# One input block loaded on a hardware queue, and index tables built on Pool, in a fused linear-attention and gated-FFN kernel

## The chip, the cores and the metric

The kernel runs on one core of a Trainium2 chip. The metric is the device time of one execution in microseconds (us), taken as the median of several executions. The span in a profile, from the first to the last instruction, is about 1.8 us shorter than that time.

Names in profile lines: PE is the matmul engine (TensorE) and PEld its weight loads, DVE is VectorE, ACT is ScalarE, POOL is GpSimd, SP is SyncE. An engine's name with a "q" behind it (SPq, ACTq, POOLq) is its sequencer, for instance where it issues a DMA. L115 is line 115 of that kernel; lines shift by a few from one kernel to the next.

## The reference

The reference does linear attention with a decay per head, followed by a gated feed-forward layer. B is 4, H is 8, S is 768 and D is 64; inputs and output are fp32.

```
for each block of the sequence:
    intra = (q_b @ k_b^T * Dmask) @ v_b          # Dmask[i,j] = lam^(i-j) for i >= j, else 0
    inter = (q_b * lam^(pos+1)) @ kv_state
    out_b = intra + inter
    kv_state = lam^block * kv_state + (k_b * lam^(block-1-pos))^T @ v_b

x    = out, transposed to (B*S, H*D) = (3072, 512)
gate = sigmoid(x @ w_gate)                       # 512 -> 1536
val  = x @ w_val
y    = (gate * val) @ w_out                      # 1536 -> 512
```

The kernel works in bf16 with fp32 sums, and in six steps of 128 positions ("step 0" is the block 0 of the change).

## The kernel before

The start is what the change touches. Pool issues nearly all loads, and its DMA casts fp32 to bf16 on the way. The q of batches 0 and 1 goes another way: it comes as fp32 over the hardware queues of ScalarE and Sync, and an engine casts it afterwards. VectorE builds the index tables (`ip1`, 1 to 128 along the row, and `p1`, 1 to 128 down the partitions) by doubling, a transpose and four offset adds.

```python
    lam1 = const.tile([1, H], FP32, tag="lam1")
    nc.sync.dma_start(out=lam1, in_=lam.partition_broadcast(1))
    # ... cut: weights' tiles, load() and load_w(), which issue casting DMAs on Pool ...
    q01 = [const.tile([128, H, D], FP32, tag=f"q{b}f", name=f"q{b}f") for b in range(2)]
    nc.scalar.dma_start(out=q01[0], in_=q[0, :, 0:C, :].rearrange("h s d -> s h d"))
    nc.sync.dma_start(out=q01[1], in_=q[1, :, 0:C, :].rearrange("h s d -> s h d"))
    # ... cut: tiles ...
    nc.vector.memset(ip1[:, 0:1], 1.0)
    w = 1
    while w < C:
        nc.vector.tensor_scalar_add(ip1[:, w:2 * w], ip1[:, 0:w], float(w))
        w *= 2
    loc = const.tile([128, 32], FP32, tag="loc")
    nc.vector.transpose(loc, ip1[:, 0:32])
    p1 = const.tile([128, 1], FP32, tag="p1")
    for lo in range(0, 128, 32):
        nc.vector.tensor_scalar_add(p1[lo:lo + 32], loc[lo:lo + 32, 0:1], float(lo))
    # ... cut: jn, ident, tri from ip1 and p1 ...
    load(0, "k", 0, 2)
    load(0, "k", 2, 4)
    load(0, "q", 2, 3)
    load(0, "q", 3, 4)
    load(0, "v", 0, 1)
    # ... cut: more v, gate and value weights, in the order of need ...
```

TensorE begins with filler matmuls (`idle(n)`), which keep it busy while it waits for data, and then does step 0: it transposes q and k (`piece_tq0`, `piece_tk0`), multiplies them (`piece_s`), VectorE masks the product (`piece_m`), and so on until the first gate matmul. The output stores all go out on Sync. The stores of step 0 are cut in two parts for some tiles, and the last tile of all is stored in two unequal parts, so that the very last store carries only 64 KB:

```python
    def piece_po(n, tt):
        # ... cut: 12 matmuls into po ...
        nc.scalar.copy(ob, po)
        parts = 2 if n == 0 and tt < 2 else 1
        rows = 128 // parts
        for i in range(parts):
            lo = tt * S + n * C + i * rows
            nc.sync.dma_start(out=out[lo:lo + rows, :], in_=ob[i * rows:(i + 1) * rows, :])

    def piece_last(n, tt):
        # ... cut: for columns 0 to 384 and 384 to 512: matmuls; ScalarE copies the first part, VectorE the second ...
            nc.sync.dma_start(out=out[tt * S + n * C:tt * S + (n + 1) * C, lo:hi], in_=ob[:, lo:hi])
```

Of the kernel before, what the change touches and what calls it, by code (L numbers as in the profile page):

```python
# [7 lines left out]
FP32 = mybir.dt.float32  # L8
BF16 = mybir.dt.bfloat16
# [6 lines left out]
def kernel(  # L16
# [11 lines left out]
    nc = tc.nc  # L28

    B, H, S, D = q.shape  # L30
    C = 128
# [9 lines left out]
    const = ctx.enter_context(tc.tile_pool(name="const", bufs=1))  # L41
    qkv = ctx.enter_context(tc.tile_pool(name="qkv", bufs=4))
# [26 lines left out]
    Q, K, V = {}, {}, {}  # L69

    def load(n, what, b0, b1):
        sl = slice(n * C, (n + 1) * C)
        for c in what:
            lst, src = {"q": (Q, q), "k": (K, k), "v": (V, v)}[c]
            if n > 1 and c != "v":
                lst[n] = qkv.tile([128, 2, B, HP, D], BF16, tag=c + "b", name=c + "b")
                for e in range(2):
                    nc.gpsimd.dma_start(  # L78
                        out=lst[n][:, e].rearrange("p b y d -> p (b y) d"),
                        in_=src[:, e::2, sl, :].rearrange("b y s d -> s (b y) d"))  # L80
                continue
            if n == 1 and c != "v":
                if n not in lst:
                    lst[n] = qkv.tile([128, 2, B * H * D // 2], BF16, tag=c + "b", name=c + "b")
                if b0 == 0:
                    nc.gpsimd.dma_start(
                        out=lst[n][:, 0].rearrange("p (x d) -> p x d", d=D),
                        in_=src[b0:b1, :, sl, :].rearrange("b h s d -> s (b h) d"))
                else:
                    for e in range(2):  # L90
                        nc.gpsimd.dma_start(
                            out=lst[n][:, 1].rearrange("p (e x d) -> p e x d", e=2, d=D)[:, e],
                            in_=src[b0:b1, e::2, sl, :].rearrange("b y s d -> s (b y) d"))
                continue
            if n not in lst:
                lst[n] = qkv.tile([128, B, H, D], BF16, tag=c + "b", name=c + "b")
            nc.gpsimd.dma_start(  # L97
                out=lst[n][:, b0:b1],
                in_=src[b0:b1, :, sl, :].rearrange("b h s d -> s (b h) d"))
# [13 lines left out]
    q01 = [const.tile([128, H, D], FP32, tag=f"q{b}f", name=f"q{b}f") for b in range(2)]  # L113
    nc.scalar.dma_start(out=q01[0], in_=q[0, :, 0:C, :].rearrange("h s d -> s h d"))
    nc.sync.dma_start(out=q01[1], in_=q[1, :, 0:C, :].rearrange("h s d -> s h d"))  # L115
    Q[0] = qkv.tile([128, B, H, D], BF16, tag="qb", name="qb")
    nc.scalar.preload_act_table_set("natural_log_exp_and_others")
    ident = const.tile([128, 128], BF16, tag="ident")
# [2 lines left out]
    ip1 = const.tile([128, C], FP32, tag="ip1")  # L121
# [2 lines left out]
    nc.vector.memset(zero, 0.0)  # L124
    nc.vector.memset(ones, 1.0)
    Sb = stp.tile([128, B, HP, D], BF16, tag="Sb", name="Sb")
    nc.vector.memset(ip1[:, 0:1], 1.0)
    w = 1
    while w < C:
        nc.vector.tensor_scalar_add(ip1[:, w:2 * w], ip1[:, 0:w], float(w))  # L130
        w *= 2
    loc = const.tile([128, 32], FP32, tag="loc")
    nc.vector.transpose(loc, ip1[:, 0:32])
    p1 = const.tile([128, 1], FP32, tag="p1")
    for lo in range(0, 128, 32):
        nc.vector.tensor_scalar_add(p1[lo:lo + 32], loc[lo:lo + 32, 0:1], float(lo))
    for i, base in enumerate((0.0, float(C))):
        nc.vector.tensor_scalar(out=jn[:, i:i + 1], in0=p1, scalar1=-1.0, scalar2=base,
                                op0=ALU.mult, op1=ALU.add)
    nc.vector.tensor_scalar(out=ident, in0=ip1, scalar1=p1, scalar2=None, op0=ALU.is_equal)  # L140
    nc.vector.tensor_scalar(out=tri, in0=ip1, scalar1=p1, scalar2=None, op0=ALU.is_ge)

    load(0, "k", 0, 2)
    load(0, "k", 2, 4)
    load(0, "q", 2, 3)
    load(0, "q", 3, 4)
# [12 lines left out]
    def idle(n):  # L159
        for i in range(n):  # L160
            nc.tensor.matmul(wm, lhsT=zero[:, :C], rhs=zero, start=True, stop=True,
                             skip_group_check=True)

    idle(4)
    lamp = ps_at.tile([128, H], FP32, name="lamp", tag="ps")
    nc.tensor.matmul(lamp, lhsT=ones, rhs=lam1, start=True, stop=True)
    lnl = const.tile([128, H], FP32, tag="lnl")
# [9 lines left out]
    pk = const.tile([128, H], FP32, tag="pk")  # L177
    nc.scalar.activation(pk, lnl, AF.Exp, scale=jn[:, 0:1])
    nc.scalar.copy(Q[0][:, 1], q01[1])
    kds = const.tile([128, H], FP32, tag="kds")  # L180
    nc.scalar.activation(kds, lnl, AF.Exp, scale=jn[:, 1:2])
    dec = const.tile([128, HP], FP32, tag="dec")
# [21 lines left out]
    def make_mask(u):  # L204
        nc.vector.tensor_tensor(
            out=mask[:, u::2, :], in0=tri.unsqueeze(1).to_broadcast([128, HP, C]),
            in1=pk[:, u::2].unsqueeze(2).to_broadcast([128, HP, C]), op=ALU.mult)
# [42 lines left out]
    def transpose_pair(out, x, b, g):  # L250
        nc.tensor.transpose(out, x[:, b, 2 * g:2 * g + 2, :].rearrange("p h d -> p (h d)"), ident)
# [7 lines left out]
    def piece_tq0(bs, then=None):  # L259
        tq = ps_at.tile([128, 2, 2, 2 * C], BF16, name="tq", tag="ps")  # L260
        for b in bs:
            if (0, b // 2) not in QS:
                QS[0, b // 2] = trsb.tile([128, 2, 2, 2, C], BF16, tag="QS", name="QS")
            for g in range(HP):
                transpose_pair(tq[:, b % 2, g // 2, g % 2 * C:g % 2 * C + C], Q[0], b, g)
        if then:
            then()
        for b in bs:
            nc.vector.tensor_tensor(out=QS[0, b // 2][:, :, b % 2].rearrange("p e x c -> p e (x c)"),
                                    in0=tq[:, b % 2], in1=lamq0_e, op=ALU.mult)  # L270

    def piece_tk0(bp):
        tk = ps_at.tile([128, 2, 2, 2 * C], BF16, name="tk", tag="ps")
        for i in range(2):
            for g in range(HP):
                transpose_pair(tk[:, i, g // 2, g % 2 * C:g % 2 * C + C], K[0], 2 * bp + i, g)
        KS[0, bp] = trsb.tile([128, 2, 2, 2, C], BF16, tag="KS", name="KS")
        for i in range(2):
            cp = nc.vector.tensor_copy if bp == 0 and i == 0 else nc.scalar.copy
            cp(KS[0, bp][:, :, i].rearrange("p e x c -> p e (x c)"), tk[:, i])  # L280
# [20 lines left out]
    def piece_s(n, bs, pool=ps_at, tag="ps"):  # L301

        for b in bs:
            bp, i = b // 2, b % 2
            sp = [pool.tile([128, HP, C], FP32, name=f"sp{u}", tag=tag) for u in range(2)]
            for hp in range(HP):
                for u in range(2):
                    us = slice(u * 64, (u + 1) * 64)
                    nc.tensor.matmul(sp[u][:, hp, :], lhsT=KS[n, bp][us, hp // 2, i, hp % 2, :],  # L309
                                     rhs=QS[n, bp][us, hp // 2, i, hp % 2, :],  # L310
                                     start=(hp == 0), stop=(hp == HP - 1), skip_group_check=True)
            SP[n, b] = sp
# [176 lines left out]
    def piece_po(n, tt):  # L489
        po = ps_ff.tile([128, DM], FP32, name="po", tag="ff")  # L490
        for ft in range(NFT):
            nc.tensor.matmul(po, lhsT=HT[n, ft][:, tt * 128:(tt + 1) * 128],  # L492
                             rhs=WO[:, ft, :], start=(ft == 0), stop=(ft == NFT - 1))
        ob = osb.tile([128, DM], FP32, tag="ob", name="ob")
        nc.scalar.copy(ob, po)  # L495
        parts = 2 if n == 0 and tt < 2 else 1
        rows = 128 // parts
        for i in range(parts):
            lo = tt * S + n * C + i * rows
            nc.sync.dma_start(out=out[lo:lo + rows, :], in_=ob[i * rows:(i + 1) * rows, :])  # L500
# [2 lines left out]
    load_gv(1, GW)  # L503
    load_gv(2, GW)

    idle(6)
    nc.vector.tensor_copy(Q[0][:, 0], q01[0])
    piece_tq0([0])
    make_mask(0)
    idle(1)  # L510
    piece_tq0([1])
    piece_tk0(0)
    make_mask(1)
    idle(1)
    piece_s(0, [0])
    piece_m(0, 0)
    piece_s(0, [1])
# [111 lines left out]
    load(3, "qkv", 0, B)  # L629
    gvh(1, 1, *range(NFT))  # L630
    piece_po(0, 0)
    piece_po(0, 1)
    piece_po(0, 2)
    t(2, 0)
    t(2, 1)
# [72 lines left out]
```

## Time and profile before

| | before |
|---|---|
| median of 3 runs | 227.5 us (227.39 to 227.57) |
| span of the profiled run | 225.7 us |
| TensorE busy | 218.7 us, 97% |
| k transposes of step 0 start | 7.48 us |
| first masked eviction (VectorE) starts | 9.08 us |
| first gate matmul starts | 15.04 us |
| end of the last PSUM copy to end of span | 2.66 us |

The list of waits of TensorE in the kernel before has four entries that are no small change. The columns are the instruction that waited, what released it, us in total, times, longest.

```profile
PE wm L161 <- DVE zero L124: 1.2, 1, 1.2
PE tk L251 <- DMA kb<-in_k_dram: 0.7, 1, 0.7
PE tq L251 <- DMA qb<-in_q_dram: 0.5, 1, 0.5
PE sp L309 <- DMA KR<-kb: 0.4, 1, 0.4
```

The timeline of the kernel before shows where these lie. The columns are start, duration, engine, line, operation, output and inputs, count, and in brackets the idle time before it and what ended it.

```profile
1.26 2.43 POOL L97 DMA_DIRECT2D kb<-in_k_dram  x2 [0.81 <-POOLq L692]
1.32 2.61 DVE L130 TENSOR_SCALAR ip<-ip 128x1 f32<-128x1 f32 x7
...
7.48 0.62 PE L251 MATMUL tk<-ident,kb 128*128 128x128 bf16 x8 [0.70 <-DMA kb<-in_k_dram]
...
9.08 2.48 DVE L211 TENSOR_TENSOR MT<-sp,mask 128x512 bf16<-128x512 f32 x4
...
15.04 0.81 PE L443 MATMUL gp<-XT,WG 128*128 128x384 bf16 x4
...
74.41 0.62 PE L309 MATMUL sp<-QS,KR 64*128 64x128 bf16 x16 [0.42 <-DMA KR<-kb]
```

VectorE spends 2.61 us on the seven doubling adds. TensorE waits 0.70 us for the k that Pool loads. After 17 us it waits once, for the transposed k of step 2 at 74.41 us.

The DMA view of the kernel before, for 4 to 5 us and for 7 to 8 us, shows a dip and the full rate. A packet of these loads reads 256 bytes; it writes 128 as bf16 on Pool's queue (q0) and 256 as fp32 on Sync's (q1).

```profile
DMA packets 547, 0.08 MB, mean 85 GB/s; under 512 B 547, under 2 KB 547, under 8 KB 547
...
q0 software_dynamic: 414, 0.05, 82.6%
q1 hardware_dynamic: 133, 0.03, 20.8%
```

```profile
DMA packets 1233, 0.16 MB, mean 157 GB/s; under 512 B 1233, under 2 KB 1233, under 8 KB 1233
```

```profile
222.77 0.29 DVE L486 COPY ob<-po 128x128 f32<-128x128 f32 x1 [9.63 <-PE po L481]
```

VectorE's last copy ends at 222.77 + 0.29 = 223.06 us. The group of the two stores ends at 223.42, and one store takes 0.33 us to issue, so the last one started at 223.09: 0.03 us after its data was ready.

### The profile page before, as it was taken

The page shows a single profiled execution, that of the slowest core. Times are in us where ns is not written, and L with a number is a line of the kernel's source. Part 1 is how long each engine was busy: PE and PEld are TensorE (multiplying, and loading weights), DVE is VectorE, ACT ScalarE, POOL GpSimd, SP SyncE. Part 2 cuts the span into 40 slices and gives each one's busy share as a digit, 9 for nine tenths or more (in the row PEclk, how much of TensorE's full clock was granted, in tenths as well). Part 3 has the DMA queues.
Part 4 walks back from the last instruction along what each step waited for, and adds up shares of the span by engine and source line. Part 5 has one row for each costly group of instructions (what it writes and reads, how often), then busy time and mean ns, then how long its engine had stood idle before and what let it go on. Part 6 is the DMA issues. An engine that isn't in the chain of part 4 may idle for free.

```text
span 225.7 us, 4301 instructions
## 1 busy us (share of the span) xinstructions
PE 218.7 (97%) x1766; PEld 114.7 (51%) x1766; DVE 106.2 (47%) x194; ACT 79.1 (35%) x150; POOL 77.0 (34%) x74
## 2 busy tenths in 40 slices
PE   7699999999999999999999999999999999999994
PEld 2355454888854455444445444446444445444443
DVE  7898647585422622435742345742334840333300
ACT  5454234344422225333115333225333225333221
POOL 8987657983294007940005950000000000000000
PEclk9999999999999999999999999999999999999999
DMA  8999999999999994999621999921820012100022
GB/s 117 154 173 196 188 176 154 143 181 172 156 127 149 229 205 131 167 151 147 24 96 46 148 157 143 66 95 50 180 54 0 0 49 93 49 0 0 0 93 97
DMA packets 105718, 25.71 MB, mean 114 GB/s; under 512 B 95842, under 2 KB 102754, under 8 KB 105698
## 3 DMA queue, kind: packets, MB, share of 16 engines
q0 software_dynamic: 81232, 13.90, 93.0%
q1 hardware_dynamic: 23426, 11.28, 23.4%
q10 hardware_dynamic: 1040, 0.26, 0.5%
q8 instruction: 14, 0.23, 0.5%
q14 instruction: 6, 0.05, 0.1%
HBM read 28.31 MB, written 6.29 MB: 153 GB/s over the span
## 4 chain that ended last, share of the span: by engine, by line
PE 66%; DMA 20%; POOL 9%; SPq 2%; issue 1%; DVE 0%; POOLq 0%
PE po L492 22%; PE gp L429 18%; PE vp L435 18%; DMA qb<-in_q_dram 6%; DMA WV<-in_moe_w_val_dram 5%; DMA KR<-kb 5%; DMA kb<-in_k_dram 5%; SPq L242 2%; PE sp L309 2%; POOL WG L103 2%; PE op L321 2%; POOL WV L103 2%; POOL vb L97 2%; PE po L481 1%; POOL kb L97 1%; PE op L333 1%
## 5 line engine op out<-in xcount | busy, mean ns | idle before, releaser
L438 DVE TENSOR_TENSOR ht<-sg,vp 128x512 bf16<-128x512 bf16 x54 | 37.1, 687 | 65.8 <-PE vp L435 65.8
L492 PE MATMUL po<-WO,ht 128*128 128x512 bf16 x276 | 61.9, 379 | 0.0
L429 PE MATMUL gp<-XT,WG 128*128 128x512 bf16 x216 | 55.5, 379 | 0.0
L435 PE MATMUL vp<-XT,WV 128*128 128x512 bf16 x216 | 55.4, 379 | 0.0
L432 ACT ACTIVATE sg<-gp 128x512 bf16<-128x512 f32 x54 | 32.2, 597 | 59.1 <-PE gp L429 59.1
L492 PEld LDWEIGHTS <-ht 128*128 128x128 bf16 x276 | 26.2, 98 | 31.0
L435 PEld LDWEIGHTS <-WV 128*128 128x128 bf16 x216 | 21.1, 98 | 25.5
L429 PEld LDWEIGHTS <-WG 128*128 128x128 bf16 x216 | 20.7, 98 | 24.8
L495 ACT COPY ob<-po 128x512 f32<-128x512 f32 x23 | 13.5, 586 | 52.7 <-PE po L492 50.9
L213 DVE TENSOR_TENSOR MT<-sp,mask 128x512 bf16<-128x512 f32 x40 | 25.1, 682 | 7.1 <-PE sp L309 7.1
L394 POOL TENSOR_TENSOR sd<-Sb,dec 128x512 f32<-128x512 bf16 x8 | 8.1, 1035 | 40.1 <-DVE Sb L420 40.0
L464 PE MATMUL gp<-XT,WG 128*128 128x256 bf16 x96 | 14.4, 273 | 0.0
L470 PE MATMUL vp<-XT,WV 128*128 128x256 bf16 x96 | 14.4, 273 | 0.0
L474 DVE TENSOR_TENSOR ht<-sg,vp 128x256 bf16<-128x256 bf16 x24 | 10.0, 420 | 8.6 <-PE vp L470 8.6
L467 ACT ACTIVATE sg<-gp 128x256 bf16<-128x256 f32 x24 | 9.2, 384 | 13.0 <-PE gp L464 11.8
L97 POOL DMA_DIRECT2D vb<-in_v_dram x10 | 12.8, 1281 | 2.5 <-DMA kb<-in_k_dram 1.0
L385 POOL TENSOR_TENSOR kd<-kb,kds 128x1024 bf16<-128x1024 bf16 x6 | 11.3, 1904 | 5.8 <-DMA kb<-in_k_dram 5.8
L420 DVE TENSOR_TENSOR Sb<-cp,sd 128x512 bf16<-128x512 f32 x8 | 5.2, 686 | 15.5 <-PE cp L413 15.5
L348 ACT CAST XT<-op 128x512 bf16<-128x512 f32 x19 | 9.9, 598 | 2.1 <-PE op L321 2.0
L464 PEld LDWEIGHTS <-WG 128*128 128x128 bf16 x96 | 9.2, 98 | 1.7 <-issue 0.2
L470 PEld LDWEIGHTS <-WV 128*128 128x128 bf16 x96 | 9.4, 98 | 1.1
L78 POOL DMA_DIRECT2D qb<-in_q_dram x8 | 9.4, 1182 | 0.0
(87 smaller groups left out, 160.0 us busy)
## 6 DMA issues: line engine op xcount, KB each, us to landing
out_dram<-ob SPq DMA_DIRECT2D x21, 256.0 KB, 2.5
kb<-in_k_dram POOLq DMA_DIRECT2D x11, 256.0 KB, 11.1
qb<-in_q_dram POOLq DMA_DIRECT2D x9, 256.0 KB, 10.0
vb<-in_v_dram POOLq DMA_DIRECT2D x4, 512.0 KB, 14.6
WO<-in_moe_w_out_dram POOLq DMA_DIRECT2D x3, 512.0 KB, 10.0
WG<-in_moe_w_gate_dram POOLq DMA_DIRECT2D x5, 256.0 KB, 9.1
WV<-in_moe_w_val_dram POOLq DMA_DIRECT2D x5, 256.0 KB, 9.7
qb<-in_q_dram POOLq DMA_DIRECT2D x4, 128.0 KB, 8.8
```

Of the source, the lines that this page charges most:

```text
L97: nc.gpsimd.dma_start(out=lst[n][:, b0:b1], in_=src[b0:b1, :, sl, :].rearrange("b h s d -> s (b h) d"))
L213: nc.vector.tensor_tensor(out=out.rearrange("p (e x) c -> p e x c", e=2), in0=x.rearrange("p (e x) c -> p e x c", e=2), in1=mask.rearrange ...
L385: nc.gpsimd.tensor_tensor(out=KD[n][:, e], in0=K[n][:, e], in1=kds[:, e::2].unsqueeze(1).unsqueeze(3).to_broadcast([128, B, HP, D]), op=AL ...
L429: nc.tensor.matmul(gp, lhsT=WG[:, mt, fs], rhs=x[:, mt, :], start=(mt == 0), stop=(mt == NMT - 1))
L432: nc.scalar.activation(sg, gp, AF.Sigmoid)
L435: nc.tensor.matmul(vp, lhsT=WV[:, mt, fs], rhs=x[:, mt, :], start=(mt == 0), stop=(mt == NMT - 1))
L438: nc.vector.tensor_mul(HT[n, ft], sg, vp)
L464: nc.tensor.matmul(gp[:, cs], lhsT=WG[:, mt, fs], rhs=x[:, mt, cs], start=(mt == 0), stop=(mt == NMT - 1))
L470: nc.tensor.matmul(vp[:, cs], lhsT=WV[:, mt, fs], rhs=x[:, mt, cs], start=(mt == 0), stop=(mt == NMT - 1))
L474: nc.vector.tensor_mul(HT[n, ft][:, cs], sg[:, cs], vp[:, cs])
L492: nc.tensor.matmul(po, lhsT=HT[n, ft][:, tt * 128:(tt + 1) * 128], rhs=WO[:, ft, :], start=(ft == 0), stop=(ft == NFT - 1))
L495: nc.scalar.copy(ob, po)
```

## The change

The intent: let TensorE start on k earlier and take work off VectorE. The k of batch 0 comes as fp32 over Sync's hardware queue behind q1, and ScalarE casts it. Pool's first load then carries only the k of batch 1. Two iotas on Pool, behind that load, replace the table building on VectorE. Fillers and masks near the start are reordered to suit, and one output store of step 0 is no longer cut in two.

```diff
     nc.sync.dma_start(out=q01[1], in_=q[1, :, 0:C, :].rearrange("h s d -> s h d"))
+    k0 = const.tile([128, H, D], FP32, tag="k0f", name="k0f")
+    nc.sync.dma_start(out=k0, in_=k[0, :, 0:C, :].rearrange("h s d -> s h d"))
+    K[0] = qkv.tile([128, B, H, D], BF16, tag="kb", name="kb")
     # ... cut ...
-    nc.vector.memset(ip1[:, 0:1], 1.0)
-    w = 1
-    while w < C:
-        nc.vector.tensor_scalar_add(ip1[:, w:2 * w], ip1[:, 0:w], float(w))
-        w *= 2
-    loc = const.tile([128, 32], FP32, tag="loc")
-    nc.vector.transpose(loc, ip1[:, 0:32])
+    load(0, "k", 1, 2)
     p1 = const.tile([128, 1], FP32, tag="p1")
-    for lo in range(0, 128, 32):
-        nc.vector.tensor_scalar_add(p1[lo:lo + 32], loc[lo:lo + 32, 0:1], float(lo))
+    nc.gpsimd.iota(p1, pattern=[[0, 1]], base=1, channel_multiplier=1, allow_small_or_imprecise_dtypes=True)
+    nc.gpsimd.iota(ip1, pattern=[[1, C]], base=1, channel_multiplier=0, allow_small_or_imprecise_dtypes=True)
     # ... cut ...
-    load(0, "k", 0, 2)
     load(0, "k", 2, 4)
     # ... cut ...
-    idle(4)
+    idle(2)
     # ... cut ...
     nc.scalar.copy(Q[0][:, 1], q01[1])
+    nc.scalar.copy(K[0][:, 0], k0)
     # ... cut ...
-        parts = 2 if n == 0 and tt < 2 else 1
+        parts = 2 if n == 0 and tt < 1 else 1
     # ... cut ...
-    idle(6)
+    idle(4)
     nc.vector.tensor_copy(Q[0][:, 0], q01[0])
+    make_mask(0)
     piece_tq0([0])
-    make_mask(0)
-    idle(1)
+    make_mask(1)
+    idle(3)
     piece_tq0([1])
+    idle(2)
     piece_tk0(0)
-    make_mask(1)
-    idle(1)
     piece_s(0, [0])
```

## The prediction

> **What bounds the kernel now.** From about 17 us to the end TensorE is full: after that the list of waits names one wait of it, 0.4 us at 74.4 us for the transposed k of step 2. Only the start of the full stretch, and that wait, can move. Two things pace the first 17 us.
> (a) The DMA stream. In 1 us windows the DMA share dips to 1.03 (85 GB/s) at 4 to 5 us and is full (about 155 GB/s of bf16) from 6 us. q0 and q1 (hardware queues) took 3.2 and 3.9 us to land; the first k (two batches, Pool), issued at 1.26, freed TensorE at 7.47. TensorE later waits for q of batches 2 and 3 (10.35, 11.26), v (13.06, 13.95) and gate weights (14.57). The chain that ended last follows it up to 74.4 us.
> (b) VectorE: index tables until 5.5, then busy 8.14 to 16 us.
>
> **Removed, added, moved.**
> - Off VectorE: eight table steps (2.67 us), transpose 0.20, offset adds 0.62. The q0 cast (5.48 before) can start at about 4.0.
> - On Pool, before its second load: two iotas and a library reload. No iota is in the trace; a 128x512 two-input Pool instruction took 1.03 us, and I estimate 0.4 to 1.0 us for the pair. The same reload before Pool's first tensor operation left a gap of at most 0.1 us (33.8 to 33.9).
> - One k batch leaves Pool's queue (first issue 1.22, becomes 0.88 us) for Sync's, behind q1, into the dip: about 0.7 us of idle DMA is filled. The Trainium skill, "DMA: Bandwidth & Descriptors", section "Queues, rings and completion order", says each engine round-robins between queue rows, so k0 and Pool's k1 should overlap, and the dip has room.
> - On ScalarE: one cast, 0.60 us, behind the q1 cast (ends 6.22): k0 ready at about 6.8.
> - One filler matmul and one output store fewer (off the chain).
>
> **What reaches the end.** k transposes at about 6.9 instead of 7.47. But VectorE must wait for the decay factors pk (ScalarE, 5.7), then do mask, scale, mask, scale, k copy (2.6 us): copy at 7.9 instead of 8.14, first masked eviction 8.9 instead of 9.08. So VectorE gains only 0.2 us. The gate matmul (15.04) waits on v of batch 2 and its eviction; with the stream 0.6 to 1.0 us earlier and VectorE 0.2, it starts 0.3 to 0.6 us earlier. The wait at 74 us shrinks if the stream gains more than TensorE. Sum: 0.4 to 1.0 us.
>
> **Predicted: 226.8 us, 226.0 to 227.5.** Faster by over 2%: 0.01; within 2%: 0.96; slower: 0.03.
>
> **What would show it.** k0 lands at 5.7 to 6.3; both iotas end before 3.6; the DMA dip at 4 to 5 us is gone; k transposes near 6.9; first gate matmul at 14.4 to 14.8; the wait at 74 us 0 to 0.4 us; the rest unchanged.
>
> **What would make it wrong.** The reload before the iotas costs microseconds: the Trainium skill, "GPSIMD Engine Reference", section 2.1, gives about 6 us for a first call to a freshly loaded library; nothing in this trace shows that. Then tables, ScalarE's lambda powers and later Pool loads slip: 229 to 232. Or Pool's second load, delayed by the iotas, opens a new DMA gap, and the wait at 74 us eats the gain.[...]

## More of the kernel before

The end of the kernel before, from the timelines of Sync and VectorE (the two were asked for one by one). The two last stores are one group, x2:

```profile
222.60 0.82 SPq L487 DMA_DIRECT2D out_dram<-ob  x2
```

## The result, and the profile after

| | before | after |
|---|---|---|
| median | 227.53 us (6 runs, 227.32 to 227.75) | 228.06 us (6 runs, 227.78 to 228.88) |
| ratio | | 1.0029, interval 1.0010 to 1.0047 |
| span of the profiled run | 225.7 us | 226.1 us |
| k transposes start | 7.48 | 8.04 |
| first masked eviction starts | 9.08 | 9.61 |
| first gate matmul starts | 15.04 | 15.34 |
| last PSUM copy ends | 223.06 | 222.88 |
| last PSUM copy to end of span | 2.66 | 3.19 |

The time is within 2%, as predicted, but it went up by about 0.5 us where a fall of 0.7 us was predicted.

The line of TensorE's list of waits in the kernel after that answers to the k transposes, same columns:

```profile
PE tk L248 <- ACT kb L176: 0.6, 1, 0.6
```

The wait for the k transposes is still there; it is now a wait for ScalarE's cast. The timeline of the kernel after shows why:

```profile
1.64 0.57 SPq L117 DMA_DIRECT2D k0f<-in_k_dram  x1
2.36 0.16 POOL L132 IOTA p<- 128x1 f32 x1
2.45 0.26 POOL L133 IOTA ip<- 128x128 f32 x1
...
7.37 0.62 ACT L176 CAST kb<-k0f 128x512 bf16<-128x512 f32 x1 [1.42 <-DMA k0f<-in_k_dram]
...
8.04 0.62 PE L248 MATMUL tk<-ident,kb 128*128 128x128 bf16 x8 [0.63 <-ACT kb L176]
...
9.61 2.48 DVE L208 TENSOR_TENSOR MT<-sp,mask 128x512 bf16<-128x512 f32 x4 [0.49 <-PE sp L306]
...
15.34 0.81 PE L440 MATMUL gp<-XT,WG 128*128 128x384 bf16 x4
...
74.22 0.62 PE L306 MATMUL sp<-QS,KR 64*128 64x128 bf16 x16
```

The iotas are as cheap as hoped: both are over by 2.71 us. But k0, issued at 1.64, lands at about 7.35, and the cast that was meant to end at 6.8 ends at 7.99. The first gate matmul is 0.30 us later than before. The wait at 74 us is gone in this run, so TensorE ends 0.18 us earlier than before, and yet the span is 0.34 us longer. The DMA view of the kernel after, for 4 to 5 us and for 5 to 6 us:

```profile
DMA packets 832, 0.19 MB, mean 192 GB/s; under 512 B 832, under 2 KB 832, under 8 KB 832
...
q1 hardware_dynamic: 700, 0.18, 105.6%
q0 software_dynamic: 132, 0.02, 25.6%
```

```profile
DMA packets 867, 0.17 MB, mean 165 GB/s; under 512 B 867, under 2 KB 867, under 8 KB 867
...
q0 software_dynamic: 437, 0.06, 85.2%
q1 hardware_dynamic: 430, 0.11, 77.0%
```

In GB/s the dip at 4 to 5 us is filled (85 became 192). In packets it rose from 547 to 832 and then gave the gain back: the kernel before moved 1042 packets from 5 to 6 us, this one 867. By 8 us of the span the kernel before had finished 5915 packets of these loads, this one 5785. (I counted these in the trace's DMA records.)

The end of the kernel after, from the timelines of Sync and of VectorE:

```profile
222.42 1.20 SPq L484 DMA_DIRECT2D out_dram<-ob  x2
```

```profile
222.59 0.29 DVE L483 COPY ob<-po 128x128 f32<-128x128 f32 x1 [9.63 <-PE po L478]
```

The last copy ends at 222.88. The two stores now span 1.20 us instead of 0.82: the last one ends at 223.62 and started at 223.29, so 0.41 us after its data was ready, with Sync otherwise idle. Before, it was 0.03 us. Nothing in the diff is near this place in time.

### The profile page after: what moved, and what is told of

Read it like the earlier page. It is cut to its first block, busy times and chain, and to the rows that moved or that the text cites. A ratio compares the mean times of both kernels' runs of the same rounds, so it can differ in the third digit from the quotient of the medians.

```text
span 226.1 us, 4288 instructions
## 1 busy us (share of the span) xinstructions
PE 218.3 (97%) x1765; PEld 114.7 (51%) x1765; DVE 104.3 (46%) x181; ACT 79.9 (35%) x151; POOL 77.1 (34%) x76
## 4 chain that ended last, share of the span: by engine, by line
PE 93%; DMA 3%; DVE 1%; ACT 1%; SPq 0%; issue 0%
PE po L489 27%; PE gp L426 21%; PE vp L432 21%; PE gp L461 5%; PE gp L440 5%; PE vp L467 5%; PE sp L306 3%; PE op L318 3%; DMA k0f<-in_k_dram 3%; PE op L330 1%; PE cp L410 1%; PE po L478 1%; DVE MT L208 1%; PE tk L248 0%; ACT kb L176 0%; ACT XT L358 0%
## 5 line engine op out<-in xcount | busy, mean ns | idle before, releaser
L461 PE MATMUL gp<-XT,WG 128*128 128x256 bf16 x96 | 14.4, 273 | 0.0
L467 PE MATMUL vp<-XT,WV 128*128 128x256 bf16 x96 | 14.4, 272 | 0.0
```

Source lines behind the costliest of these rows:

```text
L461: nc.tensor.matmul(gp[:, cs], lhsT=WG[:, mt, fs], rhs=x[:, mt, cs], start=(mt == 0), stop=(mt == NMT - 1))
L467: nc.tensor.matmul(vp[:, cs], lhsT=WV[:, mt, fs], rhs=x[:, mt, cs], start=(mt == 0), stop=(mt == NMT - 1))
```

## The experiments

Two things needed an explanation: where the predicted gain at the start went, and where the extra half microsecond at the end came from. These were the rivals.

- For the start: (1) k0's load finds no idle DMA time, so what it brings early delays Pool's stream by as much; against (2) VectorE's tables or the iotas, not the loads, set the time; against (3) the hardware queue goes first and Pool's packets wait until it has drained (this is called G in one expectation).
- For the end: (4) a pause sits at a fixed place in Sync's stream of instructions, and the added load moved the last store behind it; against (5) chance, a bad run or a bad chip; against (6) something that k0 itself does, since it is a large load on the same queue.

In the expectations these have letters: A is (1) as lateness of k0, B puts the cost at the iotas (part of 2), C at the fillers that the change takes away near the start, D is (5), E is (4), F is (6), G is (3).

The sets are the order in which the runs were made. The runs of a set shared a chip, except e3, which had its own; ratios are always to the kernel before of the same rounds.

### First set: repeats, and one part of the change at a time

**r1_after_again** is the changed kernel, unedited.

> The changed kernel, unedited, for a second trace. Theory A (late k0: TensorE's full stretch starts 0.3 us late, whatever the run): k0 lands again 5.5 to 6 us after its issue, the first gate matmul starts at 15.2 to 15.5, ratio 1.001 to 1.005. Theory D (the loss lies in what varies from run to run: the wait for the transposed k near 74 us and the last stores): the start is as in the first trace, but the wait at 74 us or the time from TensorE's last matmul to the end differs from the first trace by 0.3 us or more.

Measured: 228.17 us against 227.41, ratio 1.0026 (1.0009 to 1.0043). Last copy to last store again 0.40 us, last copy to end of span 3.25 us. The k transposes began at 7.55 and the first gate matmul at 14.92, both earlier than in the first profile, but TensorE then waited 0.7 us at 74 us. So the end repeats within 0.06 us, and the start varies from run to run by some tenths. Chance (5) is out for the end.

**r2_before_again** is the kernel before, unedited.

> The kernel before, unedited, against itself: ratio 0.999 to 1.001. First gate matmul at 15.0 to 15.1. Theory D expects the wait near 74 us and the tail after TensorE's last matmul to differ from the first trace by some 0.3 us; theory A expects them the same within 0.1 us.

Measured: 227.41 us, ratio 1.0001 (0.9989 to 1.0013); copy to store 0.03 us, copy to end 2.65 us. From 4 to 5 us this run moved 807 packets where the first profile had 547. Of the dip that the prediction rested on (686 packets below the full 1233), 260 were an accident of one profile.

**e1_iotas_only** takes k0 out of the changed kernel and leaves the iotas, the new order of fillers and masks, and the uncut store.

```diff
-    k0 = const.tile([128, H, D], FP32, tag="k0f", name="k0f")
-    nc.sync.dma_start(out=k0, in_=k[0, :, 0:C, :].rearrange("h s d -> s h d"))
-    K[0] = qkv.tile([128, B, H, D], BF16, tag="kb", name="kb")
-    load(0, "k", 1, 2)
+    load(0, "k", 0, 2)
-    nc.scalar.copy(K[0][:, 0], k0)
```

> The changed kernel with k of batch 0 back on Pool (one load of two batches, then the iotas). Theory A (k0's late landing on Sync's queue is the cost): the k transposes start at 7.4 to 7.6 again, the first gate matmul at 15.0 or earlier, ratio to the kernel before 0.998 to 1.000. Theory B (the iotas or the library reload hold up Pool's descriptors): Pool's first packets move at 4.7 instead of about 4.0 us even without k0, the k transposes start at 8.0 or later, ratio 1.002 or more. Theory C (fewer early fillers[...] is the cost): ratio stays at 1.003.

Measured: 227.35 us, ratio 0.9992 (0.9980 to 1.0004). The timeline of this kernel:

```profile
6.91 0.62 PE L244 MATMUL tk<-ident,kb 128*128 128x128 bf16 x8 [0.21 <-DMA kb<-in_k_dram]
...
8.48 2.48 DVE L204 TENSOR_TENSOR MT<-sp,mask 128x512 bf16<-128x512 f32 x4 [0.49 <-PE sp L302]
...
14.79 0.81 PE L436 MATMUL gp<-XT,WG 128*128 128x384 bf16 x4
```

Without k0 the k transposes start at 6.91, which is where the prediction had put them with k0. The first masked eviction came 0.60 us earlier than in the kernel before, the first gate matmul only 0.25 us earlier: in between TensorE waits for q, v and gate weights from Pool's stream, and the first of these waits ended at 10.09 us instead of 10.35. So the iotas do not cost time, and what VectorE's tables cost is at most these 0.25 us: (2) does not explain where the gain went. C is out as well, for this kernel has the same fillers as the changed one and is no slower than the kernel before.

**e2_k0_only** leaves k0 and puts the table building back on VectorE.

```diff
+    nc.vector.memset(ip1[:, 0:1], 1.0)
+    w = 1
+    while w < C:
+        nc.vector.tensor_scalar_add(ip1[:, w:2 * w], ip1[:, 0:w], float(w))
+        w *= 2
+    # ... cut: the transpose and the four offset adds, as in the kernel before ...
-    nc.gpsimd.iota(p1, ...)
-    nc.gpsimd.iota(ip1, ...)
```

> The changed kernel with the index tables built on VectorE again and no iota on Pool; k of batch 0 still over Sync's queue. Theory A: k0 lands at 7.2 to 7.5, k transposes at 8.0, first gate matmul at 15.3 or later, ratio 1.002 to 1.006. Theory B: Pool's packets start at about 4.0 again, k0 or k1 no longer late, ratio 0.999 to 1.001.

Measured: 229.63 us, ratio 1.0101 (1.0086 to 1.0116), more than either expectation, the k transposes at 8.64 and the first gate matmul at 16.23. The kernel after orders VectorE's work for early tables; with late ones the cast of q0 (at 5.22) and everything behind it slips. Copy to store was 0.40 us here too, so the pause at the end goes with k0 on Sync and not with the iotas.

### Second set: is it k0, or one more instruction on Sync?

**t1_before_one_more** is the kernel before with one load of 32 bytes more on Sync, into a tile that nobody reads.

```diff
     nc.sync.dma_start(out=q01[1], in_=q[1, :, 0:C, :].rearrange("h s d -> s h d"))
+    for i in range(1):
+        junk = const.tile([1, H], FP32, tag=f"junk{i}", name=f"junk{i}")
+        nc.sync.dma_start(out=junk, in_=lam.partition_broadcast(1))
```

> The kernel before with one more 32-byte load on Sync's queue near the start, into a tile nobody reads. Theory E (Sync stalls some 0.4 us at a fixed place of its instruction stream; k0's extra load pushed the last store behind it): the pause before the last store's issue grows from 0.1 to 0.4 or 0.5 us, the time from TensorE's last matmul to the end grows by 0.4 to 0.6 us, ratio 1.0015 to 1.003. Theory F (the end is longer because of what k0 moves, its bytes or its lateness): nothing changes, ratio 1.000.

Measured: 228.47 us against 227.44, ratio 1.0046 (1.0034 to 1.0058). A load of 32 bytes in the first 2 us costs 1.0 us at the median. Sync's timeline of this kernel at the end:

```profile
222.56 1.22 SPq L490 DMA_DIRECT2D out_dram<-ob  x2
```

The two last stores span 1.22 us, the last one starts 0.42 us after its data, and copy to end is 3.49 us instead of 2.66. This accounts for 0.83 us of the 1.03; the first gate matmul was 0.25 us later than in the first profile of the kernel before. Rival (6), that k0's size is at fault, is out: a load of 32 bytes does the same.

**t2_after_one_fewer** is the changed kernel with one store fewer on Sync: the last cut store is stored whole.

```diff
-        parts = 2 if n == 0 and tt < 1 else 1
+        parts = 1
```

> The changed kernel with the last split store made whole too, so Sync has one store fewer. Theory E: the stall falls behind the last store again, the end is 0.5 us shorter than in the changed kernel, ratio 0.999 to 1.0012. Theory F: ratio stays at 1.002 to 1.004.

Measured: 227.32 us against 227.44, ratio 0.9994 (0.9979 to 1.0008). Copy to store 0.03 us, copy to end 2.71 us. Taking one instruction off Sync brings the end back.

**t3_after_two_more** is the changed kernel with two loads of 32 bytes behind k0 on Sync (the same edit as t1, `range(2)`).

> The changed kernel with two more 32-byte loads on Sync's queue behind k0's. Theory E: the stall moves ahead of the last two stores, into the time in which Sync waits for TensorE anyway, so more instructions cost less: the end is 0.4 to 0.5 us shorter than in the changed kernel, ratio 0.999 to 1.0015. A plain count of Sync's work (each store issue costs time at the end) expects the same ratio as the changed kernel or a higher one, 1.003 or more.

Measured: 227.91 us, ratio 1.0024 (1.0006 to 1.0043), higher than theory E expected. Copy to store is back at 0.03 us: with two more instructions the pause is gone again. Copy to end is 3.02 us, not 2.66, and that is a second effect. At its end Sync checks each semaphore that its DMAs raise, one wait after the other. In this kernel the last store's semaphore stood third in the row instead of last, so once it had landed there were still waits to go through, 0.06 us each. In t1 it stood second, which explains why t1's end is the longest of all.

**x1_k0_on_scalar** moves k0 to ScalarE's queue, behind q0.

```diff
-    nc.sync.dma_start(out=k0, in_=k[0, :, 0:C, :].rearrange("h s d -> s h d"))
+    nc.scalar.dma_start(out=k0, in_=k[0, :, 0:C, :].rearrange("h s d -> s h d"))
```

> The changed kernel with k0 on ScalarE's hardware queue behind q0, not on Sync's behind q1. Theory E: the end is as in the kernel before. On the front: if a hardware transfer simply runs ahead of Pool's queue (theory G: Pool's packets start only when the hardware queues are nearly drained, so k0 shifts Pool's stream by its own 1.0 us), Pool's stream stays 1 us late whichever hardware queue carries k0, and k0 lands 4.5 to 5.5 us after issue; ratio 0.9995 to 1.002. If the lateness comes from standing behind q1 on one ring, k0 lands before 6.2 us and the k transposes start before 7.2.

Measured: 227.12 us, ratio 0.9990 (0.9978 to 1.0002). The end is back to 0.03 and 2.65 us; Sync has one record fewer. k0 is issued 0.4 us earlier and lands 5.3 us after its issue, so the k transposes start at 7.22 and the first gate matmul at 14.84.

### Third set: the pause at another place, and a test of how the queues share

**t4_after_eight_more** is the changed kernel with eight such tiny loads (`range(8)`). Eight is chosen because the semaphores of Sync's DMAs go round in eights (107, 109, 110, 113 and 115 to 118 in the trace), so the last store's semaphore is the one it is in the changed kernel.

> The changed kernel with eight more 32-byte loads on Sync's queue, so that the last store has the same semaphore as in the changed kernel (they go round in eights) but Sync's fixed stall falls far ahead of the last stores. Theory E: the pause before the last store's issue is 0.1 us again, the time from TensorE's last matmul to the end 2.7 to 2.8 us instead of 3.3, and the kernel with eight loads MORE is faster than the changed one: ratio 0.999 to 1.001. A plain cost per Sync instruction: ratio 1.004 or more. If the middle run with two more was slow for another reason than the place of its last store's semaphore in the final list of waits, this one is slow too: 1.002 or more.

Measured: 227.63 us against 227.32, ratio 1.0016 (0.9996 to 1.0035). Copy to store 0.03 us, copy to end 2.64 us: with eight loads more than the changed kernel the end is as short as before the change. The time does not show it clearly and falls between the two expectations. In the profiled run the start was late (first gate matmul 15.40), and TensorE waited 0.5 us for VectorE at 25.3 us.

**x2_k0_on_scalar_again** is x1, unedited, on another chip.

> k0 on ScalarE's queue once more, to see whether it beats the kernel before clearly: ratio 0.998 to 1.000, k0 lands 5.0 to 5.5 us after its issue, first gate matmul 14.7 to 15.0.

Measured: 227.33 us against 227.32, ratio 1.0002 (0.9988 to 1.0016). So x1's 0.1% is not a gain to rely on; it is a tie with the kernel before.

**x3_k0_k1_on_scalar** goes further: k of both batches 0 and 1 as fp32 on ScalarE's queue, no k for Pool to load before batch 2.

```diff
-    nc.sync.dma_start(out=k0, in_=k[0, :, 0:C, :].rearrange("h s d -> s h d"))
+    nc.scalar.dma_start(out=k0, in_=k[0, :, 0:C, :].rearrange("h s d -> s h d"))
+    k1 = const.tile([128, H, D], FP32, tag="k1f", name="k1f")
+    nc.scalar.dma_start(out=k1, in_=k[1, :, 0:C, :].rearrange("h s d -> s h d"))
-    load(0, "k", 1, 2)
     nc.scalar.copy(K[0][:, 0], k0)
+    nc.scalar.copy(K[0][:, 1], k1)
-        parts = 2 if n == 0 and tt < 1 else 1
+        parts = 1
```

> k of batches 0 and 1 both on ScalarE's hardware queue, cast on ScalarE; Pool's first load is k of batches 2 and 3; one split store made whole so that the end is as in the kernel before. Theory G (the hardware queues' packets go ahead and Pool's start when they are nearly drained): Pool's first packets at about 5.5 to 6 us, one more us later than with k0 alone; all packets done by 8 us stay 6000 to 6250 as in the other runs of this chip; k1 lands near 7.3 us; ratio 0.999 to 1.003. If the dip at the handover were idle DMA time that a load can fill (the prediction), the packets done by 8 us would grow by 300 or more and the first gate matmul would start before 14.5 us.

Measured: 230.09 us, ratio 1.0162 (1.0117 to 1.0207), a plain miss for the theory called G; whether it is slower by 2% is unclear. The granted clock of its six runs was 0.978 to 0.993, that of the kernel before in the same rounds 0.999 to 1.000, so not all of the ratio need be the late k. The second half of the k transposes waited until 10.49, as the timeline shows by the cast before them:

```profile
9.82 0.62 ACT L178 CAST kb<-k1f 128x512 bf16<-128x512 f32 x1 [2.68 <-DMA k1f<-in_k_dram]
```

k1 was issued at 1.82 and landed 8.0 us later. The DMA view for 6 to 7 us and for 7 to 8 us (q10 is ScalarE's queue) shows its packets still on the way:

```profile
DMA packets 1014, 0.16 MB, mean 157 GB/s; under 512 B 1014, under 2 KB 1014, under 8 KB 1014
...
q0 software_dynamic: 800, 0.10, 158.7%
q10 hardware_dynamic: 214, 0.05, 41.0%
```

```profile
DMA packets 835, 0.16 MB, mean 162 GB/s; under 512 B 835, under 2 KB 835, under 8 KB 835
...
q10 hardware_dynamic: 433, 0.11, 82.1%
q0 software_dynamic: 402, 0.05, 77.1%
```

Pool's packets do not wait until the hardware queue has drained: from 6 to 7 us they are the greater part (800 to 214), from 7 to 8 us about half. So rival (3) is out. And the total from 7 to 8 us is 835 packets, where Pool's queue alone moves 1233. The hardware queues alone are slower than that too, as the kernel after shows from 3 to 4 us:

```profile
DMA packets 1067, 0.27 MB, mean 269 GB/s; under 512 B 1067, under 2 KB 1067, under 8 KB 1067
...
q1 hardware_dynamic: 808, 0.21, 95.4%
q10 hardware_dynamic: 259, 0.06, 28.2%
```

In x3 they moved 887 from 4 to 5 us, 8 of these Pool's. So 835 is below either alone, but part of the distance from 1233 may lie in the hardware queue's own packets, which write twice the bytes; I have not separated the two.

**e3_iotas_only_again** is e1, unedited, on another chip.

> The iotas without k0 once more, to see whether the half of the change that frees VectorE beats the kernel before clearly. If VectorE's tables were on the critical path: ratio 0.997 to 0.999, first gate matmul 14.5 to 14.8. If TensorE waits for the DMA stream whatever VectorE does: k transposes and the first masked eviction are earlier than in the kernel before by 0.3 us or more, but the first gate matmul by 0.3 at most, and the ratio is 0.9985 to 1.0005.

Measured: 227.50 us against 227.28, ratio 1.0021 (0.9995 to 1.0046), with one run at 228.88 among six. The first gate matmul began at 14.84 (14.79 in e1), but the time does not show the gain. In e1's profile TensorE met a new wait of 0.3 us for VectorE further on; the repeat met one of 0.4 us. The iotas alone are worth at most about a tenth of a per cent in e1, and nothing that two sets agree on.

### Fourth set: the pause without k0, and the pause removed once more

The cause at the end still rested on one clean pair. This set asked for the missing cross: iotas only, but with Sync's stream of the changed kernel.

**t5_iotas_one_more** is e1 with one load of 32 bytes on Sync behind q1 (the edit of t1).

> The iotas without k0, and one 32-byte load on Sync's queue in the place where the changed kernel issues k0: Sync's instruction stream and the last store's semaphore are then as in the changed kernel, but k goes by Pool. Theory E (the fixed stall before the last store is the loss): the last store's issue pauses 0.4 to 0.5 us, the time from TensorE's last matmul to the end is 3.2 to 3.4 us, ratio 1.0015 to 1.0035. If k0's transfer itself, at the start, is the loss: end 2.8 us, ratio 0.999 to 1.001.

Measured: 227.79 us against 227.48, ratio 1.0016 (1.0004 to 1.0028). Copy to store 0.41 us, copy to end 3.39 us. There is no k0 here, the last PSUM copy was early (it ended at 222.28 us, 0.6 us before that of the changed kernel), and the end still costs 0.7 us.

**t6_after_one_fewer_again** is t2, unedited, on another chip.

> The changed kernel with one store fewer on Sync once more, beside the changed kernel on the same chip. Theory E: 0.4 to 0.8 us below the changed kernel, ratio to the kernel before 0.9985 to 1.001, end 2.7 to 2.8 us.

Measured: 227.07 us against 227.48, ratio 0.9982 (0.9970 to 0.9994). Sync's timeline at the end:

```profile
221.96 0.82 SPq L484 DMA_DIRECT2D out_dram<-ob  x2
```

The two stores take 0.82 us again. With one store taken off Sync the change is no longer a loss: over the two chips 0.9994 and 0.9982, and on this one faster than both kernels.

**r3_after_third** is the changed kernel once more, on the same chip as t5 and t6.

> The changed kernel for a third trace, to be compared with the run of one store fewer on the same chip. Ratio to the kernel before 1.0015 to 1.004, end 3.2 to 3.4 us.

Measured: 227.84 us, ratio 1.0019 (1.0002 to 1.0037); copy to store 0.40 us, copy to end 3.19 us. t6 is 0.77 us below it at the median, and 0.50 us of this is the difference of the two ends (3.19 against 2.69); in the profiled pair the first gate matmul was also earlier in t6 (14.87 against 15.53).

### All ends in one table

The trace has a record for each wait and DMA issue of Sync. I counted them in every trace, and looked for the pause: the longest gap near the end of Sync's stream for which it waits on nothing that the trace shows.

| kernel | Sync's records in all | the last store is record | last copy to last store, us | last copy to end, us |
|---|---|---|---|---|
| e1, e3, x3 | 92 | 78 | 0.03 | 2.64 to 2.71 |
| before, r2, t2, t6, x1, x2 | 93 | 79 | 0.03 | 2.65 to 2.71 |
| after, r1, r3, e2, t5 | 94 | 80 | 0.40 to 0.41 | 3.19 to 3.39 |
| t1 | 95 | 81 | 0.42 | 3.49 |
| t3 | 96 | 82 | 0.03 | 3.02 |
| t4 | 102 | 88 | 0.03 | 2.64 |

In all fifteen traces with 92 to 95 records the pause is 0.45 to 0.47 us long (the ordinary gap there is 0.04 to 0.09 us, and is part of it) and stands before record 80, whatever that record is. In those with 92 or 93 it comes after the last store, where Sync has to wait for the landing anyway. With 94 it hits the last store itself. With 95 it hits the wait just before it. With 96 or 102 records, record 80 is an earlier store, for whose data Sync waits 1.45 us or more anyway, and the pause drops out of sight.

## Why the prediction was right or wrong

**Right: the class, and nearly so what fills TensorE.** The prediction said within 2%, and that only the start, the wait at 74 us and nothing else of the full stretch could move. After 17 us TensorE's list of waits has one entry or none in every profile. But in r2, r3, e1, e3 and t4 it is another one, 0.3 to 0.5 us for VectorE at about 25 us.

**Right: the iotas.** "Both iotas end before 3.6" was kept with room: 0.16 and 0.26 us, over by 2.71. The risk that the prediction named from the Trainium skill, "GPSIMD Engine Reference", section 2.1 (about 6 us more for the first call to a freshly loaded kernel of Pool's), did not come: in the kernel after, Pool's first load ends at 2.27 us, the two records of the reload (MODIFY_POOL_CONFIG) start at 2.27 and 2.30, and the first iota starts at 2.36.

**Half right: VectorE is not where the gain is.** e1, without k0, moved the first masked eviction 0.60 us earlier, where the prediction gave VectorE 0.2, and the gate matmul 0.25 us. So this half of the change brought what gain there was. It came with an earlier k: the same load of k by Pool landed at 6.87 to 7.20 us in e1, e3 and t5, and at 7.36 to 7.70 in before, r2 and t1. Why, I have not taken apart.

**Wrong: "into the dip: about 0.7 us of idle DMA is filled".** This is the step that failed at the start. The dip of 547 packets per us was to a good part chance: r2 and t1, with the same loads, moved 807 and 787 in that microsecond. And k0 did not fill it: the seven traces with k0 on Sync moved 763 to 832 packets there, e1, e3 and t5 without k0 835, 896 and 707. The time in which a hardware queue and Pool's queue both have work is a slow one: 867 packets from 5 to 6 us in the kernel after and 835 from 7 to 8 us in x3, against 1233 for Pool alone. A load of 1024 packets more on the hardware side makes this stretch longer: from 5 to 6 us the seven traces with k0 on Sync moved 867 to 1000 packets, before, r2 and t1 moved 1042 to 1108. The packets finished by 8 us:

| kernels | traces | finished by 8 us, mean (range) | first gate matmul, mean (range) |
|---|---|---|---|
| k as before, tables on VectorE (before, r2, t1) | 3 | 6171 (5915 to 6332) | 15.08 (14.92 to 15.29) |
| k as before, iotas (e1, e3, t5) | 3 | 6207 (6153 to 6268) | 14.77 (14.68 to 14.84) |
| k0 on Sync, iotas (after, r1, r3, t2, t3, t4, t6) | 7 | 5973 (5785 to 6159) | 15.13 (14.87 to 15.53) |
| k0 on ScalarE, iotas (x1, x2) | 2 | 6287 (6179 to 6394) | 14.95 (14.84 to 15.05) |

The iotas bring the first gate matmul forward by about 0.3 us, and k0 on Sync gives about 0.36 us back. At 1233 packets per us, 234 packets (6207 less 5973) are 0.19 us, an estimate from the numbers above; so the slower stream would account for about half of it. That is argued and not shown: x1 and x2 had finished as many packets as the iota kernels, and their gate matmul was still 0.18 us later. The rest I have not taken apart. The ranges overlap between before and after, and no claim finer than "the gain is gone" rests on them.

**Wrong as a consequence: "k0 lands at 5.7 to 6.3", "k transposes at about 6.9", "first gate matmul at 14.4 to 14.8".** k0 landed at 7.35 in the first profile and at 6.9 to 7.0 in r1, r3 and t2; the k transposes began at 7.55 to 8.04 in the four of these; the first gate matmul at 14.87 to 15.53 in all seven traces. The landing times that the prediction had to go by were those of q0 and q1 (3.2 and 3.9 us), which shared the engines almost only with each other. k0 shares with Pool's stream and took 5.2 to 5.7 us in these four.

**The wait at 74 us** was predicted at 0 to 0.4 us and was 0, 0.7 and 0 in the three traces of the changed kernel. It varies likewise in the kernel before (0.4 and 0), so it explains differences between profiles and none between kernels.

**Wrong, and as large as the whole loss: "one output store fewer (off the chain)" and "the rest unchanged".** The prediction counted the stores as free, and it did not count k0's load as an instruction of Sync at all. Sync's last store is on the chain, and where it stands in Sync's stream decides whether a pause of about 0.4 us falls before it or behind it. The change put one record more in front of it in total (a load and a wait more, a store fewer), which is exactly one too many. Last copy to end of span: 3.21 us as the mean of after, r1 and r3, 2.66 us of before and r2, so 0.55 us. The medians differ by 0.53 us in the rounds of the first result, 0.76 and 0.36 us in the two other sets. Of the 1.26 us between the predicted 226.8 and the measured 228.06, about 0.7 is thus the gain at the start that did not come, and 0.55 the end. That it is the position and not k0 was shown in both directions: t1 and t5 make the pause without k0, t2, t6, t3 and t4 remove it with k0 on Sync.

Of the 0.55 us, the pause itself is 0.38 (0.41 less 0.03). The remaining 0.17 goes with a longer time from issue to landing of the same 64 KB store, in the list of DMA issues first of the kernel before and then of the kernel after:

```profile
out_dram<-ob SPq DMA_DIRECT2D x1, 64.0 KB, 1.7
```

```profile
out_dram<-ob SPq DMA_DIRECT2D x1, 64.0 KB, 1.9
```

Why it lands later is open: in after, r1, r3, e2 and t5, where the pause is directly before the store, it landed in 1.87 to 2.08 us, but in t1, where a wait stands between, in 1.74.

**Open: what the pause is.** A fixed place in one engine's stream suggests that Sync fetches its next block of instructions there. The Trainium skill, "Runtime: NRT & Kernel Launch", section "Instruction fetch mechanics", says instructions are refilled in blocks of 16 KiB and that crossing such a border is "mostly hidden". The trace has packets of 8 KB and of 16 KB on two queues that it calls instruction queues, and one of them goes with the place. In all seventeen traces an 8 KB packet starts 1.08 to 1.71 us after the end of Sync's record 79. In t3 and t4, where record 79 comes early (it ends at 221.05 and 193.21 us), this packet is early too, at 222.22 and 194.37; in the others it is at 223.3 us or later. But in the fifteen traces that show the pause it starts 0.6 to 1.3 us after the pause is over, so Sync does not wait for this packet to arrive. That a block of instructions is asked for at this place is likely; that this is what makes the pause is only argued. The place and the cost are shown.

## What to carry to other kernels

When a change adds or removes an instruction on the engine that issues the last store, look at the end of the profile as well as at the place of the change: compare the time from the last copy to the issue of the last store, and if it grew, add or drop one harmless instruction there and see whether it moves. A dip of the DMA in one profile is no idle time until a second profile shows it too, and while loads on a hardware queue ran beside the casting stream on Pool's queue, fewer packets moved than with Pool's queue alone (835 from 7 to 8 us in x3, against 1233), so count packets rather than GB/s. An early gain counts only as far as the next thing that the stream delivers: 0.60 us at the first mask became 0.25 us at the first gate matmul.

## What the Trainium skill lacked or had wrong

- "Runtime: NRT & Kernel Launch", section "Instruction fetch mechanics": if the pause is such a border, "mostly hidden" misses the case where it falls just before the last store. The runs show a pause of 0.45 to 0.47 us before Sync's 80th record in each of fifteen traces, exposed in after, r1, r3, e2, t5 and t1, where the end is 0.5 to 0.8 us longer. That it is a fetch is not shown; the packet that goes with the place has 8 KB, where the page has blocks of 16 KiB.
- No page that I read says that the end of an engine's program goes through its DMA semaphores one wait after another, so that the place of the last store's semaphore in that row matters: 0.06 us for each wait behind it, last copy to end 3.02 us in t3 (third in the row) against 2.64 us in t4 (last).
- "DMA: Bandwidth & Descriptors", section "Queues, rings and completion order", says that each engine takes turns between the queues it has work for. The trace agrees from 7 to 8 us of x3 (433 and 402 packets); from 6 to 7 us it is 214 and 800, and whether the hardware queue had less work ready then is open. The page does not say that the total falls while a hardware queue and Pool's queue take turns: 835 packets from 7 to 8 us there, against 1233 of Pool's queue alone and 887 and 1067 of the hardware queues alone, all of 256 bytes read.
- "GPSIMD Engine Reference", section 2.1: the 6 us for the first call to a freshly loaded kernel did not show; the first iota started 0.09 us after Pool's load had ended. Nothing in the trace says that the iota's code was freshly loaded, so the figure is not shown to be wrong.
